# Waiting for the last two stores on the queues that issued them, in a one-token attention and MLP layer

## The chip, the cores and the metric

The kernel runs on one core of a Trainium2 chip. The metric is the device time of one execution in microseconds (us). Before the change it is 100.47 us, the median of three runs that lie between 100.42 and 100.51 us.

## The reference

One token `x` of 1024 values goes through a layer norm, and then through two branches whose results are added to it: grouped attention with 32 query heads and 4 key and value heads over the last 4096 positions of a cache, and an MLP with 3584 hidden units that has a second layer norm of its own. Everything is stored in bf16.

```python
W = min(4096, max(256, Sk // 4))                     # 4096 of 65536 positions
q = (x @ wq).reshape(B, Sq, Hq, Dh)                  # 32 heads of 128
k, v = k_cache[:, :, Sk - W:, :], v_cache[:, :, Sk - W:, :]   # each head repeated 8 times
p = softmax(q @ k.T * Dh ** -0.5)
A = (p @ v).reshape(B, Sq, Hq * Dh) @ wo
B = gelu(layernorm(x) @ w1 + b1) @ w2 + b2
out = x + A(xn) + B(xn)                              # xn = layernorm(x)
```

## The kernel before

The work is bound to weights and caches that are read once: 39.86 MB come from HBM, and the output is one row of 1024 values. Four SBUF buffers (`slot`) are loaded in turn by SyncE (SP): the key window, `wq`, the two halves of `w1`, the value window, the two halves of `w2`, and at the end the 32 rows of `wo` in pieces. TensorE (PE) multiplies the rows as they land. VectorE (DVE) and ScalarE (ACT) transpose and copy the keys, and VectorE adds most rows of `w2` up. GpSimd (POOL) builds masks in the first part and is not needed for arithmetic after that.

The end of the work goes like this. The last rows of `wo` land, 32 small matmuls (line 227, with helper loads at line 219) add them into the PSUM tile `acc`, VectorE copies 288 columns of it to the SBUF tile `res` (line 569) and ScalarE the other 224 (line 570). Then two DMAs of 1 KB each write the output: one half is issued by SyncE (`out0`) and the other half by ScalarE (`out1`), both by the helper whose `dma_start` call is at line 213. They are the last two operations of the plan, and their numbers are given to `emit` as `done`.

`Plan.emit` turns a list of operations into instructions with semaphores. Each engine has a counter (`pe_count`, `dve_count` and so on) that it raises when an operation on which another engine depends is finished. Each DMA has a semaphore of its own that is 16 when all of it has landed. At the end, GpSimd sets all of them back to zero, so that the program can run again:

- at line 111 it waits until VectorE's and ScalarE's counters have their last values, which is when `res` is complete;
- at line 112 it clears the list `used`: all semaphores of loads and the counters of PE, GpSimd and SyncE;
- at lines 113 and 114 it waits for the two stores;
- at line 115 it clears the list `ends`: the counters of VectorE and ScalarE and the semaphores of the two stores.

SyncE and ScalarE have nothing more to do after they issued their stores, and VectorE and PE, whose instructions are put in blocks of their own behind this (`dve_main`, `pe_main`), have nothing after `res` and the last matmul.

Of the kernel before, what the change touches and what calls it, by code (L numbers as in the profile page):

```python
# [14 lines left out]
class Plan:  # L15
# [11 lines left out]
    def emit(self, done):  # L27
        nc, ops = self.nc, self.ops
        writer, readers, deps = {}, {}, []
        for n, (eng, fn, r, w, dma, over) in enumerate(ops):  # L30
            need = set()
            for k in over:
                need.update((m, False) for m in readers.get(k, ()))
            for k in r:
                if k in writer:
                    need.add((writer[k], True))
            for k in w:
                if k in writer:
                    need.add((writer[k], True))
                need.update((m, False) for m in readers.get(k, ()))  # L40
            keep = set()
            for m, after_write in need:
                if m == n:
                    continue
                same = ops[m][0] == eng and ops[m][4] is None and dma is None
                if same and (eng == "pe" or not after_write):
                    continue
                keep.add(m)
            deps.append(keep)
            for k in r:  # L50
                readers.setdefault(k, []).append(n)
            for k in w:
                writer[k] = n
                readers[k] = []
        clock = {e: {} for e in self.engines}
        snap, waits, ordinal, count = [], [], [], {e: 0 for e in self.engines}
        for n, (eng, fn, r, w, dma, _) in enumerate(ops):
            c, mine = clock[eng], []
            for m in sorted(deps[n], reverse=True):
                lane = ("dma", m) if ops[m][4] is not None else ops[m][0]  # L60
                if c.get(lane, -1) >= ordinal[m]:
                    continue
                mine.append(m)
                for key, v in snap[m].items():
                    if c.get(key, -1) < v:
                        c[key] = v
                c[lane] = max(c.get(lane, -1), ordinal[m])
            waits.append(mine)
            ordinal.append(count[eng])
            count[eng] += 1  # L70
            snap.append(dict(c))
        wanted = {m for mine in waits for m in mine if ops[m][4] is None}
        wanted.update(m for m in range(len(ops)) if m in done)
        sems = {e: nc.alloc_semaphore(f"{e}_count") for e in ("pe", "pool", "sp")}
        used, ends = list(sems.values()), []
        value, ticks = {}, {e: 0 for e in self.engines}
        for e in ("dve", "act"):
            sems[e] = nc.alloc_semaphore(f"{e}_count")
            ends.append(sems[e])
        for n in done:  # L80
            value[n] = (nc.alloc_semaphore(f"dma{n}"), 16)
            ends.append(value[n][0])
        for n, (eng, fn, r, w, dma, _) in enumerate(ops):
            if dma is not None:
                if n in done:
                    continue
                value[n] = (nc.alloc_semaphore(f"dma{n}") if dma is True else dma, 16)
                used.append(value[n][0])
            elif n in wanted:
                ticks[eng] += 1  # L90
                value[n] = (sems[eng], ticks[eng])

        def put(n):
            eng, fn, r, w, dma, _ = ops[n]
            lanes = {}
            for m in waits[n]:
                s, v = value[m]
                if id(s) not in lanes or lanes[id(s)][1] < v:
                    lanes[id(s)] = (s, v)
            for s, v in lanes.values():  # L100
                self.engines[eng].wait_ge(s, v)
            i = fn()
            if i is not None and n in value:
                i.then_inc(value[n][0], value[n][1] if dma is not None else 1)

        own = [("dve", mybir.EngineType.DVE), ("pe", mybir.EngineType.PE)]
        for n, o in enumerate(ops):
            if o[0] not in ("dve", "pe"):
                put(n)
        for e in ("dve", "act"):  # L110
            nc.gpsimd.wait_ge(sems[e], ticks[e])
        nc.clear_and_free_semaphores(used)
        for s, v in [value[m] for m in done]:
            nc.gpsimd.wait_ge(s, v)
        nc.clear_and_free_semaphores(ends)
        never = {}
        for e, _ in own:
            never[e] = self.engines[e].alloc_register(f"{e}_never")
            self.engines[e].reg_mov(never[e], 0)
            self.engines[e].br(f"{e}_main")  # L120
        for e, kind in own:
            nc.enter_bb(f"{e}_main", valid_engines=[kind])
            back = self.engines[e].mark_branch_hint_location()
            for n, o in enumerate(ops):
                if o[0] == e:
                    put(n)
            self.engines[e].br_eq(never[e], 1, f"{e}_main", f"{e}_last").branch_hint(back)
            nc.enter_bb(f"{e}_last", valid_engines=[kind])
            self.engines[e].nop()
# [475 lines left out]
```

## Time and profile before

| | us |
|---|---|
| median of three runs | 100.47 (100.42 to 100.51) |
| the profiled execution, its own time | 100.62 |
| the profiled execution, span from the first to the last instruction of the kernel | 98.83 |
| time of that execution that lies around the span | 1.79 |
| last matmul of `acc` raises PE's counter, from the span's start | 96.93 |
| SyncE issues its store | 97.38 to 97.65 |
| ScalarE issues its store | 97.40 to 97.88 |
| ScalarE's store has landed | 98.50 |
| SyncE's store has landed | 98.68 |
| GpSimd's last clear (line 115) | 98.79 to 98.83 |

The page of the profile lists busy time by engine; instructions that only wait, branch, clear semaphores or issue DMAs are not counted as busy and stand in the views by line with a q behind the engine's name (SPq, POOLq). The landing times are from the trace's records of semaphore updates: a store's semaphore reaches its full value there.

The records of semaphore updates go on after the kernel's last instruction. The kernel's own semaphores have the numbers 99 to 129. Number 2 isn't one of them; it is raised in groups of nine, once just before the kernel's first instruction, once around its end, and once after all semaphores have been set back to zero. The prediction calls these updates marks.

### The profile page before, as it was taken

How to read it: one execution, taken by the hardware profiler on the slowest of the kernel's cores; microseconds unless marked ns; L12 is line 12 of the kernel's file. 1: busy time of each engine (PE TensorE's matmuls, PEld its weight loads, DVE VectorE, ACT ScalarE, POOL GpSimd, SP SyncE). 2: the span in 40 equal slices, each digit the busy share in tenths (PEclk: the TensorE clock that was granted, in tenths of full speed). 3: DMA queues.
4: the chain of work that ended last, by engine and by line, in shares of the span. 5: the costliest groups of instructions: out<-in, count | busy, mean ns of one | idle time of the engine just before them, and what ended most of it. 6: DMA issues, size and time to landing. Idle time of an engine off the chain costs nothing.

```text
span 98.8 us, 961 instructions
## 1 busy us (share of the span) xinstructions
PE 57.2 (58%) x323; PEld 16.2 (16%) x220; DVE 73.9 (75%) x75; ACT 30.7 (31%) x29; POOL 10.0 (10%) x22
## 2 busy tenths in 40 slices
PE   0032040598200699960899586667670999594792
PEld 0022000123000233410202121212210111110130
DVE  0023776999999999999102677899999999999431
ACT  0050000089999899992001075100000000000001
POOL 0072580000000680000000000000000000000000
PEclk9999999999985556997558999999999589999999
DMA  3999979999999999999799999999998999999970
GB/s 50 448 418 451 464 328 458 441 511 438 424 424 405 395 453 453 395 441 464 338 424 424 418 441 413 463 424 429 487 418 383 431 431 424 424 424 405 405 265 1
DMA packets 3132, 39.86 MB, mean 403 GB/s; under 512 B 438, under 2 KB 444, under 8 KB 828
## 3 DMA queue, kind: packets, MB, share of 16 engines
q1 hardware_dynamic: 3082, 39.86, 95.4%
q10 hardware_dynamic: 50, 0.00, 0.0%
HBM read 39.86 MB, written 0.00 MB: 403 GB/s over the span
## 4 chain that ended last, share of the span: by engine, by line
DVE 36%; DMA 32%; PE 20%; issue 5%; SPq 2%; ACT 2%; DVEq 0%
DMA slot<-in_A_wo_dram 20%; DVE slot L334 18%; DVE kT L343 13%; DMA slot<-in_A_k_cache_dram 13%; PE qo_ps L495 10%; PE sc_ps L227 6%; PE acc L227 2%; SPq L194 2%; ACT e L450 1%; DVE eTb L454 1%; DVE m_loc L435 1%; PE acc L233 1%; DVE q_sb L388 1%; ACT sc L427 1%; DVE res L569 0%
## 5 line engine op out<-in xcount | busy, mean ns | idle before, releaser
L339 ACT COPY kT<-slot 32x1024 bf16<-32x1024 bf16 (+1 forms) x18 | 23.9, 1327 | 14.3 <-DVE slot L334 14.1
L482 DVE SCALAR_TENSOR_TENSOR run<-slot,hTf,run 128x1024 f32<-128x1024 bf16 x20 | 24.2, 1272 | 0.0
L369 PE MATMUL acc<-slot,xw 128*128 x48 | 15.7, 494 | 12.6 <-DMA slot<-in_A_wq_dram 12.2
L334 DVE STREAM_TRANSPOSE slot<-slot 128x4096 bf16<-128x4096 bf16 x4 | 17.4, 4414 | 1.2 <-DMA slot<-in_A_k_cache_dram 1.2
L343 DVE COPY kT<-slot 32x4096 bf16<-32x4096 bf16 x10 | 13.2, 1316 | 0.2
L495 PE MATMUL qo_ps<-slot,eTb 128*128 (+1 forms) x32 | 10.2, 382 | 5.1 <-issue 4.0
L227 PE MATMUL sc_ps<-slot,o 128*1 128x512 bf16 x48 | 9.1, 378 | 2.8 <-DMA slot<-in_A_wo_dram 2.8
L369 PEld LDWEIGHTS acc<-slot,xw 128*128 x48 | 5.5, 115 | 23.5 <-issue 21.1
L570 ACT CAST res<-acc 33x224 bf16<-33x224 f32 x1 | 0.3, 338 | 20.1 <-PE acc L227 20.1
L227 PE MATMUL sc_ps<-kT,qm 128*32 128x512 bf16 x32 | 6.1, 973 | 0.3 <-DVE qm L416 0.3
L495 PEld LDWEIGHTS qo_ps<-slot,eTb 128*128 (+1 forms) x32 | 3.1, 96 | 12.0 <-issue 8.7
L428 DVE COPY sc<-sc_ps 128x512 f32<-128x512 f32 x1 | 0.7, 691 | 5.7 <-PE sc_ps L227 5.7
L227 PE MATMUL sc_ps<-slot,hT 128*1 128x512 bf16 x14 | 4.7, 509 | 0.1
L538 ACT CAST o<-misc 128x32 bf16<-128x32 f32 x1 | 0.2, 186 | 14.6 <-PE misc L233 14.6
L219 PEld LDWEIGHTS <-o 128*1 128x1 bf16 x40 | 2.4, 83 | 12.4 <-issue 11.8
L233 PE MATMUL misc<-x,spread 32*128 32x8 bf16 x4 | 0.3, 168 | 6.2 <-POOL spread L255 6.2
L249 DVE MEMSET mhalf<- 128x1 f32 x1 | 0.1, 59 | 5.0 <-PEq L203 5.0
L233 PE MATMUL acc<-spread,qm 32*128 32x512 bf16 x4 | 1.6, 498 | 3.7 <-POOL qm L315 3.7
L227 PE MATMUL acc<-slot,yT 128*1 128x448 bf16 x64 | 3.4, 353 | 0.0
L427 ACT COPY sc<-sc_ps 128x512 f32<-128x512 f32 x1 | 0.6, 585 | 8.8 <-PE sc_ps L227 8.8
L251 ACT ACT_TABLE_LOAD x1 | 1.3, 1283 | 4.8 <-PEq L203 4.8
L227 PE MATMUL acc<-slot,o 128*1 128x288 bf16 (+1 forms) x32 | 2.2, 272 | 0.6 <-DMA slot<-in_A_wo_dram 0.6
(88 smaller groups left out, 46.0 us busy)
## 6 DMA issues: line engine op xcount, KB each, us to landing
slot<-in_B_w_dram SPq DMA_DIRECT2D x3, 3584.0 KB, 16.6
slot<-in_A_wo_dram SPq DMA_DIRECT2D x3, 2048.0 KB, 22.8
slot<-in_A_k_cache_dram SPq DMA_DIRECT2D x4, 1024.0 KB, 9.8
slot<-in_A_wq_dram SPq DMA_DIRECT2D x1, 4096.0 KB, 27.0
slot<-in_A_v_cache_dram SPq DMA_DIRECT2D x1, 4096.0 KB, 16.1
slot<-in_A_wq_dram SPq DMA_DIRECT2D x2, 1024.0 KB, 9.2
slot<-in_A_wq_dram SPq DMA_DIRECT2D x1, 2048.0 KB, 17.8
slot<-in_B_w_dram SPq DMA_DIRECT2D x1, 2048.0 KB, 21.5
```

The source lines that it names most:

```text
L194: return nc.sync.dma_start(out=k_sb[g:P - Hkv + g + 1:Hkv, :], in_=A_k_cache[0, g, Sk - W:Sk, :].rearrange("(r c) d -> r (c d)", r=P // Hkv))
L219: return pe.add_instruction(mybir.InstLdweights(name=nc.get_next_instruction_name(), engine=i.engine, tile_size=(P, 32), tile_position=pos ...
L227: return pe.add_instruction(mybir.InstMatmult(name=nc.get_next_instruction_name(), engine=i.engine, start_tensor_calc=start, stop_tensor_c ...
L233: op("pe", lambda: pe.matmul(out_ap, lhsT=w_ap, rhs=x_ap, start=start, stop=stop, tile_position=pos), r, w)
L251: op("act", lambda: act.activation(out=dummy[:, 0:1], in_=mhalf[0:1, 0:1], func=ACT.Exp), ("mhalf",), ("act_warm",))
L334: op("dve", lambda s=s: dve.transpose(out=scr[:, s, :], in_=k2[:, s, :]), ("k0", "k1", "k2", "k3", "slot0"), (f"scr{s}",))
L339: op("act", lambda s0=s0, s1=s1, R=R, Cd=Cd: act.copy(out=kT[32 * Cd:32 * Cd + 32, R, s0:s1, :].rearrange("p s (c j) -> p (s c) j", j=32), ...
L343: op("dve", lambda R=R, Cd=Cd: dve.tensor_copy(out=kT[32 * Cd:32 * Cd + 32, R, :, :].rearrange("p s (c j) -> p (s c) j", j=32), in_=T3[32 ...
L369: pe.matmul(acc2[:, b, :], lhsT=xw[:, bass.ds(32 * n + 512 * i, P)], rhs=slot[1 + i][:, bass.ds(1024 * n + 512 * b, 512)], start=False, st ...
L427: op("act", lambda: act.copy(out=sc[:, 512:1024], in_=sc_ps[:, 1, :]), ("sc1",), ("scs1",))
L482: op("dve", lambda: dve.scalar_tensor_tensor(out=t, in0=wap, scalar=hTf[:, c:c + 1], in1=t, op0=ALU.mult, op1=ALU.add), (key, "hTf", f"run ...
L495: return pe.matmul(qo_ps, lhsT=cols, rhs=v4[:, :, c, :], start=first, stop=last)
```

## The change

The semaphores of the two stores leave the list that GpSimd clears, and a new semaphore, `left`, enters it. SyncE and ScalarE each raise `left` by one right behind the instruction that issues their store. GpSimd no longer waits for the stores: it waits until `left` is 2, and then clears VectorE's and ScalarE's counters and `left`. SyncE and ScalarE each get one more instruction at their end, which waits until the engine's own store has landed (16) and takes the 16 back from the semaphore.

```diff
         for e in ("dve", "act"):
             sems[e] = nc.alloc_semaphore(f"{e}_count")
             ends.append(sems[e])
+        left = nc.alloc_semaphore("left")
+        ends.append(left)
         for n in done:
             value[n] = (nc.alloc_semaphore(f"dma{n}"), 16)
-            ends.append(value[n][0])
...
         nc.clear_and_free_semaphores(used)
-        for s, v in [value[m] for m in done]:
-            nc.gpsimd.wait_ge(s, v)
+        for n in done:
+            self.engines[ops[n][0]].sem_inc(left, 1)
+        nc.gpsimd.wait_ge(left, len(done))
         nc.clear_and_free_semaphores(ends)
+        for n in done:
+            s, v = value[n]
+            self.engines[ops[n][0]].wait_ge(s, v).then_inc(s, -v)
```

## The prediction

> **What bounds the kernel now.** I read the page first, then the chain of waits, then the timeline of the last microseconds, and last the lines that the diff touches.
>
> The page and the end of the chain of waits (start, length, what):
>
> ```profile
> span 98.8 us, 961 instructions
> ...
> DMA  3999979999999999999799999999998999999970
> ...
> 74.51 19.40 DMA slot<-in_A_wo_dram
> ...
> 96.86 0.45 DVE res L569
> ```
>
> The transfers are busy up to the last two slices; nothing that the diff touches can move them. The chain of the view ends with `res` at 97.31 us. What follows is the part that the diff touches: 1.52 us up to the end of the span at 98.83, and 1.79 us more that the profiled execution took (100.62) than its span.
>
> The timeline of that part (start, length, engine, line):
>
> ```profile
> 96.95 0.34 ACT L570 CAST res<-acc 33x224 bf16<-33x224 f32 x1 [20.07 <-PE acc L227]
> 97.38 0.27 SPq L213 DMA_DIRECT2D out_dram<-res  x1
> 97.40 0.48 ACTq L213 DMA_DIRECT2D out_dram<-res  x1
> ```
>
> The lines of GpSimd's end (durations in ns, then the start in us):
>
> ```profile
> L112 POOLq EVENT_SEMAPHORE_RANGE_CLEAR  x2: 92/112/132, 97.5 to 97.7; - x2
> L114 POOLq EVENT_SEMAPHORE  x1: 17/17/17, 98.5 to 98.5; - x1
> L115 POOLq DRAIN  x1: 55/55/55, 98.7 to 98.7; - x1
> L115 POOLq EVENT_SEMAPHORE_RANGE_CLEAR  x1: 47/47/47, 98.8 to 98.8; - x1
> ```
>
> GpSimd stands from 97.85 us on for the two stores. ScalarE's lands at 98.504 and GpSimd's wait at line 114 starts 0.024 later; SyncE's lands at 98.678, the drain that carries its wait starts 0.024 later (98.702 to 98.757), and the clear runs from 98.786 to 98.833. So 0.155 us lie between the last landing and the end of the span.
>
> The rest is in the records of semaphore updates, semaphore 2, in us from the span's start:
>
> ```
> marks before the kernel   -0.371 -0.337 -0.299 -0.255 -0.231 -0.120 -0.081 -0.047  0.000
> marks at its end          97.089 98.147 99.354 99.399 99.422 99.519 99.559 99.593 99.639
> marks after the clearing 100.429 100.464 100.502 100.546 100.569 100.668 100.706 100.740 100.787
> ```
>
> The first and third rows run freely, with steps of 0.02 to 0.11 us. The second row doesn't: its first mark comes 0.161 us after PE's counter got its last update (96.928), its second 0.272 after ScalarE had issued its store (97.875), its third 0.521 after GpSimd's last clear (98.833), and from there the steps are the free ones (0.045 against 0.044, 0.023 against 0.023). I read the marks as a round of the five engines in a fixed order, there and back, in which each adds its mark when it is done and has seen the one before: PE, ScalarE, GpSimd, then VectorE and SyncE in the two remaining places, SyncE at the turn, and back. That SyncE turns is inferred: it is the first engine with an instruction in the kernel, at 0.00. All other semaphores are cleared behind the fifth to ninth mark, and the last row follows. So **GpSimd's last clear and its walk of 0.521 us to the third mark set the end**; the time from the fifth mark (99.422) to the last update (100.787), 1.365 us, hangs behind it.
>
> The Trainium skill, page "Runtime: NRT & Kernel Launch", section "The ~15µs preamble/postamble breakdown", describes such a round of the five engines (44 ns a hop), here 0.371 us for eight steps, and gives about 1.5 us for waiting there until all engines are done. Here 0.81 us pass from GpSimd's last clear to the ninth mark. Taken as a fixed price behind the last instruction, whichever engine has it, its rule would leave only the shift of the span's end; that shift is worked out as a rival below.
>
> **The change part by part.**
>
> *Raising `left`.* Two instructions, on SyncE and ScalarE, behind the issue of the store. The stores themselves aren't moved or delayed. The nearest rows are the waits of these engines:
>
> ```profile
> L203 SPq EVENT_SEMAPHORE  x2: 17/17/17, 4.4 to 4.7; - x2
> L203 ACTq EVENT_SEMAPHORE  x2: 17/17/17, 4.4 to 4.7; - x2
> ```
>
> They take 0.017 us, and 0.05 to 0.09 us from start to the start of what follows. SyncE is free at 97.646 and ScalarE at 97.875, and each would stand until its landing at 98.678 and 98.504. The cover is over 0.6 us, so the cost is nothing; without cover it would be at most 0.09.
>
> *GpSimd's end.* `left` is 2 at about 97.875 + 0.06 + 0.017 = 97.95. Then come 0.024, the drain and the clear (98.833 - 98.702 = 0.131): the end is at 98.11, in place of 98.833. With the walk of 0.521 GpSimd reaches its mark at 98.63. The first clears of line 112 end at 97.85 and stay where they are; the list has two runs of numbers as before. GpSimd is no longer last.
>
> *SyncE's and ScalarE's last instructions.* Each is a wait that also takes the value back; the two rows above are of this form (they wait for and lower a semaphore), 0.017 us. Nothing of the kernel is queued behind them; only the marks wait for them. ScalarE: 98.504 + 0.024 + 0.017 = 98.545. SyncE: 98.678 + 0.024 + 0.017 = **98.719**, which becomes the last instruction of the kernel.
>
> *The walk from there to the mark.* This is the disputed size. GpSimd's is 0.521, ScalarE's 0.272, PE's 0.161 from its last update. SyncE's isn't seen: it is free at 97.646 and has only to have marked by 99.422, so anything up to 1.776 us would have been hidden. By the rows it stands between 0.161 and 0.521. I take ScalarE's 0.272, for two reasons. In the barrier at line 203 SyncE and ScalarE keep the same pace (0.092 us from a wait to the next drain on both, 0.072 and 0.076 from the second wait to what follows). And their drains take 7 and 8 ns where GpSimd's take 34 to 184, which would lengthen a walk that contains some:
>
> ```profile
> L203 POOLq DRAIN  x2: 34/38/41, 0.8 to 4.4; - x2
> L112 POOLq DRAIN  x2: 70/76/82, 97.4 to 97.6; - x2
> L589 SPq DRAIN  x1: 7/7/7, 0.0 to 0.0; - x1
> L589 ACTq DRAIN  x1: 8/8/8, 0.1 to 0.1; - x1
> ```
>
> **The sum.** SyncE's mark, the fifth: 98.719 + 0.272 = 98.991. What is late next is ScalarE: 98.545 + 0.272 = 98.817, and three free steps (0.038, 0.045, 0.023) bring it to 98.923 at the fifth mark. GpSimd's 98.63 is behind ScalarE's mark. So SyncE's own arrival sets the fifth mark, at 98.991 in place of 99.422: **0.43 us less**, of which the span shows only 0.11. Behind it 1.365 us follow as now. The profiled execution of 100.62 becomes 100.19; it lies 0.15 above the median of the runs, so the forecast for the median is 100.47 - 0.43 = **100.04 us**.
>
> **Bounds.** With PE's 0.161 for both walks, SyncE marks at 98.880: 0.54 less, 99.93 us. With GpSimd's 0.521 it marks at 99.240: 0.18 less, 100.29 us. If VectorE turned and SyncE stood fourth, one step of 0.023 would be added. The runs before spread by 0.04 to each side.
>
> **The rivals.**
>
> 1. *Every engine's walk is about GpSimd's, when it comes out of a last wait for a store* (chance 0.15). ScalarE's walk was seen only behind a DMA issue, not behind a wait. For it: GpSimd is the only engine whose walk began at such a wait. Against it: drains on GpSimd are dearer. The gain is 0.18 us, 100.29. The neighbouring reading, a fixed time behind the kernel's last instruction, gives 98.833 - 98.719 = 0.11 less, 100.36. Both are hardly to be told from no change.
> 2. *SyncE's walk is long, and its stand hid it* (chance 0.08). The mechanism: SyncE must now begin, 1.07 us later than today (98.719 against 97.646), a way to the mark that has always lain under GpSimd's wait. It decides from a walk of 0.70 us on (99.422 - 98.719); there the change gains nothing. At the limit of what today's trace can hide, 1.776 us, the mark would be at 100.495, 1.07 late: 101.54 us. In the middle of that, 1.24, it is 0.54 late, 101.01. For it: no row of SyncE's walk exists. Against it: its pace in the barrier rows is ScalarE's.
> 3. *The change doesn't do what it says* (chance 0.05): the raise of `left` waits for the store on one of the engines, or the wait and the taking back fall apart into more instructions, with GpSimd's clear again behind the landing. Then GpSimd's walk sets the end as now: 100.47, at most 0.1 to either side.
> 4. *Both walks are shorter than PE's row* (chance 0.02): below 99.93 us.
>
> **How the numbers follow.** The forecast has 0.70. A measurement of this kernel can tell about 0.2% from no change, 0.20 us. Faster by more than that: the forecast and case 4, 0.72. Within it: cases 1 and 3, 0.20. Slower: case 2, 0.08. The range takes in the forecast with its bounds and case 1's own 0.18, with 0.04 for the spread of the runs: from 99.93 - 0.04 = 99.89 to 100.29 + 0.04 = 100.33 us.
>
> **What would show it.** In the profile of the changed kernel: GpSimd's last clear near 98.1 us; a wait of SyncE at about 98.7 as the last instruction, so a span only 0.11 shorter while the time falls by about 0.43; the third mark no longer 0.52 behind GpSimd's clear but a free step behind the second; the fifth mark 0.27 behind SyncE's wait. The prediction is wrong if that last distance is over 0.5 us, if a store lands later than 1.3 us after its issue, or if the marks follow the span's end at the old distance.

## The result, and the profile after

The changed kernel takes **99.93 us** (median of five runs, 99.84 to 99.95) against 100.51 us of the kernel before beside it (100.42 to 100.67): a ratio of 0.9939 with a 95% interval of 0.9925 to 0.9954, so 0.6% faster. The forecast was 100.04 us, 0.43 less than before; 0.58 was measured. All ratios here are to the kernel before, run beside, and leave out the few executions that took over 1.5% longer than the fastest of their kernel.

The page, the end of the chain of waits and the timeline (start, length, engine and line) of the changed kernel:

```profile
span 98.6 us, 964 instructions
...
DMA  3999979999999899889799999999998999999970
```

```profile
75.74 20.58 DMA slot<-in_A_wo_dram
...
96.69 0.45 DVE res L574
```

```profile
97.21 0.27 SPq L218 DMA_DIRECT2D out_dram<-res  x1
97.23 0.48 ACTq L218 DMA_DIRECT2D out_dram<-res  x1
```

The profiled executions differ ahead of the change too: `res` begins 0.17 us earlier here, and 0.14 us of that stand already at the first transposes (15.44 in place of 15.58 us). The diff touches nothing there. Therefore everything below is counted from PE's last update of its counter, behind the last matmul (96.928 us before, 96.761 after). From there the stores are issued at 0.45 and 0.47 us in both kernels.

The lines of the changed end (durations in ns, then the start in us): the two raises of `left`, GpSimd's last clear, and the two waits that take a semaphore back.

```profile
L115 SPq EVENT_SEMAPHORE  x1: 17/17/17, 97.5 to 97.5; - x1
L115 ACTq EVENT_SEMAPHORE  x1: 17/17/17, 97.7 to 97.7; - x1
```

```profile
L117 POOLq DRAIN  x1: 62/62/62, 97.8 to 97.8; - x1
L117 POOLq EVENT_SEMAPHORE_RANGE_CLEAR  x1: 46/46/46, 97.9 to 97.9; - x1
```

```profile
L120 ACTq EVENT_SEMAPHORE  x1: 17/17/17, 98.4 to 98.4; - x1
L120 SPq EVENT_SEMAPHORE  x1: 17/17/17, 98.5 to 98.5; - x1
```

GpSimd's last clear has moved from 98.8 to 97.9 us, ahead of both landings, and the kernel's last instruction is SyncE's wait at 98.54. Each new instruction takes 17 ns. The marks, from the records of semaphore 2, in us from PE's last update, in the kernel before, the changed one, and a second run of the changed one:

```
              mark:  1     2     3     4     5     6     7     8     9   last update
before             0.161 1.219 2.426 2.471 2.494 2.591 2.631 2.665 2.711  3.859
after              0.160 1.756 1.794 1.838 1.943 1.987 2.025 2.059 2.106  3.257
after, again       0.161 1.758 1.796 1.840 1.945 1.989 2.027 2.061 2.108  3.260
```

The third mark, which hung on GpSimd, is now a free step (0.038) behind the second, and the second comes 0.140 us behind the end of ScalarE's wait (1.616). The fifth comes 0.146 behind the end of SyncE's wait (1.797), and 0.105 behind the fourth, where 0.023 is the free step: SyncE is the last to arrive. The last update comes 0.60 us earlier, about the measured gain of 0.58, while the kernel's last instruction ends only 0.11 us earlier (1.797 in place of 1.905).

That the last update stands for the program's time can be read from the profiles. In nine of the twelve of this document the execution's own time is 0.167 to 0.183 us less than the time of its last update from the span's start (100.62 against 100.787 before, 99.84 against 100.018 after). The exceptions are three kernels of the experiments: with one store on SyncE (0.04 less), with one store on ScalarE (0.64 more) and with both waits on TensorE (0.75 more).

### The profile page after: what moved, and what is told of

The parts are those of the page before. It is cut to its first block, busy times and chain, and to the rows that moved or that the text cites. A ratio compares the mean times of both kernels' runs of the same rounds, so it can differ in the third digit from the quotient of the medians.

```text
span 98.6 us, 964 instructions
## 1 busy us (share of the span) xinstructions
PE 57.2 (58%) x323; PEld 16.2 (16%) x220; DVE 73.9 (75%) x75; ACT 30.8 (31%) x29; POOL 9.9 (10%) x22
## 4 chain that ended last, share of the span: by engine, by line
DVE 36%; DMA 33%; PE 18%; issue 5%; SPq 4%; ACT 2%; DVEq 0%
DMA slot<-in_A_wo_dram 21%; DVE slot L339 18%; DVE kT L348 13%; DMA slot<-in_A_k_cache_dram 12%; PE qo_ps L500 10%; PE sc_ps L232 6%; SPq L199 2%; SPq L218 2%; ACT e L455 1%; DVE eTb L459 1%; DVE m_loc L440 1%; DVE q_sb L393 1%; ACT sc L432 1%; DVE res L574 0%; SPq L204 0%
```

## The experiments

The way from an engine's last instruction to its mark is called its walk, as in the prediction. Theory A: GpSimd walks about 0.52 us from its last instruction to its mark, whatever that instruction is; ScalarE and SyncE walk about 0.15. So what counts is which engine handles the last landing. Theory B: the 0.52 us belong to the clear that was GpSimd's last instruction. A further rival is that each half of the change has its own share. All diffs are against the changed kernel and cut to the lines that matter, and the marks are counted from PE's last update as above.

**GpSimd takes the stores back itself** (e1_pool_takes).

```diff
-        for n in done:
+        for n in reversed(done):
             s, v = value[n]
-            self.engines[ops[n][0]].wait_ge(s, v).then_inc(s, -v)
+            nc.gpsimd.wait_ge(s, v).then_inc(s, -v)
```

> GpSimd clears the counters while the stores fly, as in the changed kernel, but GpSimd itself then waits for both stores and takes their semaphores back; SyncE and ScalarE only raise left. No clear is behind the landing. Theory A (the walk to the mark depends on the engine, and GpSimd's is about 0.52 us after any last instruction): GpSimd's last wait ends 0.04 us after the last landing and its mark, the third, comes 0.52 us later; against the kernel before only the drain and the clear are saved, about 0.1 us, so -0.1%. Theory B (the 0.52 us belong to the clear that was GpSimd's last instruction): the mark comes about 0.15 us after the wait, as on SyncE and ScalarE in the changed kernel, and some 0.48 us are saved, -0.5%.

Measured: ratio 0.9985 (0.9956 to 1.0014), the last update at 3.801 us. The lines of GpSimd's end in this kernel:

```profile
L117 POOLq EVENT_SEMAPHORE_RANGE_CLEAR  x1: 46/46/46, 97.9 to 97.9; - x1
...
L120 POOLq EVENT_SEMAPHORE  x2: 17/17/17, 98.4 to 98.6; - x2
```

The clear is early, exactly as in the changed kernel, and the two waits are 17 ns each; but the second ends at 1.806 and the third mark comes at 2.371, 0.565 later. By the marks only 0.06 us of the 0.60 are gained, and the ratio can't tell that from nothing. Theory A holds, and B falls: clearing the counters while the stores fly is nearly worthless as long as GpSimd is the one that waits.

**One half of the change at a time** (e2_sp_part_alone, e3_act_part_alone). One engine takes its own store back; the other store's semaphore is waited for and cleared by GpSimd.

```diff
             value[n] = (nc.alloc_semaphore(f"dma{n}"), 16)
+        ends.append(value[done[1]][0])        # done[0] in the other run
...
-        for n in done:
-            self.engines[ops[n][0]].sem_inc(left, 1)
-        nc.gpsimd.wait_ge(left, len(done))
+        mine, its = done[0], done[1]          # done[1], done[0] in the other run
+        self.engines[ops[mine][0]].sem_inc(left, 1)
+        nc.gpsimd.wait_ge(left, 1)
+        nc.gpsimd.wait_ge(*value[its])
         nc.clear_and_free_semaphores(ends)
-        for n in done:
-            s, v = value[n]
-            self.engines[ops[n][0]].wait_ge(s, v).then_inc(s, -v)
+        s, v = value[mine]
+        self.engines[ops[mine][0]].wait_ge(s, v).then_inc(s, -v)
```

> SyncE waits for its own store and takes its semaphore back; GpSimd still waits for ScalarE's store and clears it with the other counters. Theory A and B alike: GpSimd's clear ends 0.155 us after ScalarE's landing, which is 0.17 us before SyncE's, and the third mark 0.52 us behind it: about 0.17 us less than before, -0.17%. If the whole gain came from what SyncE does, it would be 0.6 us, -0.6%.

> ScalarE waits for its own store and takes its semaphore back; GpSimd still waits for SyncE's store and clears it with the other counters. GpSimd's clear ends 0.155 us after the last landing as before, and the third mark 0.52 us behind it: no difference, 0.0%, within 0.05 us. If each half of the change had its own share, the two halves alone would add up to 0.6 us, and this one would bring some 0.4.

Measured: with SyncE's half alone a ratio of 1.0009 (0.9978 to 1.0041), with ScalarE's half alone 0.9981 (0.9941 to 1.0022). GpSimd's end in the two kernels, SyncE's half first:

```profile
L119 POOLq DRAIN  x1: 55/55/55, 98.2 to 98.2; - x1
L119 POOLq EVENT_SEMAPHORE_RANGE_CLEAR  x1: 47/47/47, 98.3 to 98.3; - x1
```

```profile
L119 POOLq DRAIN  x1: 55/55/55, 98.7 to 98.7; - x1
L119 POOLq EVENT_SEMAPHORE_RANGE_CLEAR  x1: 47/47/47, 98.8 to 98.8; - x1
```

GpSimd clears behind the landing that is left to it, and its third mark follows 0.521 us behind the clear in both (1.783 to 2.304, and 1.974 to 2.495). The last update is 0.12 us earlier than before with SyncE's half and 0.07 later with ScalarE's, where the wait for the store is now an instruction of its own ahead of the drain (it was part of the drain before). The runs can't tell the 0.12 from nothing; that figure rests on one profile. The two halves don't add up: -0.12 and +0.07 alone, -0.60 together. The gain comes only when GpSimd waits for no store at all.

**Both stores taken back by one engine** (e4 ScalarE, e5 SyncE, e8 VectorE, e9 TensorE). The two waits stand at the end of that engine's stream, for VectorE and TensorE at the end of their own blocks.

```diff
-        for n in done:
+        for n in reversed(done):
             s, v = value[n]
-            self.engines[ops[n][0]].wait_ge(s, v).then_inc(s, -v)
+            self.engines["act"].wait_ge(s, v).then_inc(s, -v)      # "sp"; "dve" and "pe" behind the nop
```

> As the changed kernel, but ScalarE takes both semaphores back and SyncE only raises left. It tests the order of the round of marks. Theory (ScalarE stands second and SyncE fifth): ScalarE's mark comes about 0.18 us after SyncE's landing, and three steps, 0.1 to 0.2 us, follow before the round has got as far as in the changed kernel: 0.15 us more than the changed kernel, 0.45 less than before, -0.45%. Rival (the place in the round doesn't matter, each engine's mark counts once): as the changed kernel, -0.6%.

> As the changed kernel, but SyncE takes both semaphores back and ScalarE only raises left; the counterpart of the run with both on ScalarE, which ended 0.14 us later than the changed kernel. Theory (SyncE's landing and walk alone set the end, and SyncE stands late in the round): as the changed kernel, -0.6%, the last update of semaphore 2 about 3.26 us after PE's last (before: 3.86, changed kernel: 3.26); ScalarE's mark early. Rival (a second wait on SyncE delays its mark, or ScalarE's landing had its own part in the end): 0.05 us to either side of that.

> As the changed kernel, but VectorE takes both semaphores back, at the end of its own block; SyncE and ScalarE only raise left. It asks whether GpSimd alone has a dear walk. Theory (GpSimd's 0.52 to 0.57 us is its own, the other engines walk in about 0.15 us behind such a wait): VectorE's mark, the fourth, comes about 0.15 us after its last wait, that is 1.95 us after PE's last update, and the last update of semaphore 2 at about 3.3 (changed kernel 3.26, before 3.86), -0.55% against before. Rival (ScalarE and SyncE are the quick ones, since they are the engines that issue DMAs, and every other engine walks like GpSimd): the fourth mark 0.52 us after the wait, at 2.32, the last update at 3.7, -0.15%.

> As the changed kernel, but TensorE takes both semaphores back, at the end of its own block. Theory (its walk is about 0.16 us, as behind its last matmul, and it stands first, so the whole round follows): first mark at 1.95 us after PE's last update, the last update of semaphore 2 at about 3.45, 0.2 later than the changed kernel, -0.4% against before. Rival (every engine but ScalarE and SyncE walks like GpSimd): first mark at 2.32, the last update at 3.85, 0.0%.

Measured, with the walk from the end of the last wait to the engine's own mark (that of GpSimd from the first experiment beside them):

```
engine     its mark   last wait ends   mark    walk    sixth mark   last update   ratio to before
ScalarE    2          1.791            1.931   0.140   2.133        3.399         0.9936 (0.9905 to 0.9967)
SyncE      5          1.791            1.934   0.143   1.978        3.248         0.9927 (0.9893 to 0.9960)
VectorE    4          1.796            1.978   0.182   2.099        3.366         0.9962 (0.9941 to 0.9983)
TensorE    1          1.835            2.069   0.234   2.305        3.854         0.9959 (0.9937 to 0.9981)
GpSimd     3          1.806            2.371   0.565   2.535        3.801         0.9985 (0.9956 to 1.0014)
```

The lines of the waits: VectorE's take 21 ns, TensorE's 51.

```profile
L135 DVEq EVENT_SEMAPHORE  x2: 21/21/21, 98.4 to 98.6; - x2
```

```profile
L135 PEldq EVENT_SEMAPHORE  x2: 51/51/51, 98.5 to 98.7; - x2
```

In each run the mark that came late was that of the engine that was given the waits, and the marks behind it up to the fifth followed in free steps (0.02 to 0.05). So the order in the round, which the prediction had inferred, is shown: TensorE, ScalarE, GpSimd, VectorE, SyncE. GpSimd alone has a walk of over 0.5 us; the others take 0.14 to 0.23. And the place matters too: the same landing on ScalarE, second in the round, gives a sixth mark 0.155 us later than on SyncE. The rival that the place doesn't matter falls by the marks (the ratios of the two, 0.9936 and 0.9927, overlap). TensorE's mark came at 2.069, 0.12 us behind the theory's 1.95 and 0.25 ahead of the rival's 2.32, and the ratio is the theory's. But the last update of its profile came at 3.854, where the theory had 3.45 and the rival 3.85. Of the 0.40 us beyond the theory only 0.12 come from the late mark; the rest lies between the ninth mark and the next row, where 1.07 us pass and in ten of the twelve profiles 0.79. That profile is of an execution that took 101.50 us where the median is 100.48, and no instruction of the kernel is left in that stretch; what the 0.28 us are stays open.

**One store in place of two** (e6 SyncE, e7 ScalarE).

```diff
-    out_v = out.rearrange("a b (t s n) -> t (a b) s n", t=2, s=16)
-    dma("sp", out_v[0], res[0:1, :].rearrange("a (s n) -> a s n", s=16), ("res_a", "res_b"), ("out0",))
-    dma("act", out_v[1], res[32:33, :].rearrange("a (s n) -> a s n", s=16), ("res_a", "res_b"), ("out1",))
-    plan.emit([len(plan.ops) - 2, len(plan.ops) - 1])
+    dma("sp", out.rearrange("a b (t n) -> t (a b n)", t=2), res[0:33:32, :], ("res_a", "res_b"), ("out0",))   # "act"
+    plan.emit([len(plan.ops) - 1])
```

> Both halves of the output in one store of two rows, issued by SyncE, which waits for it and takes it back; ScalarE issues none. Theory (the end hangs on SyncE's landing, and its packet ran 0.05 us behind ScalarE's on the same chip resource): the packet starts up to 0.05 us earlier and the landing comes 0.05 to 0.1 us earlier, so the last update of semaphore 2 comes at about 3.17 to 3.21 us after PE's last, against 3.26 in the changed kernel, -0.65 to -0.7% against before. Rival (two rows in one store take longer to issue and to land than one): the landing is 0.1 to 0.3 us later and all of it is seen at the end, -0.3 to -0.5%.

> Both halves in one store of two rows, issued by ScalarE, which waits for it and takes it back; SyncE issues none. Theory (ScalarE's store lands 1.11 us after the start of its issue against 1.30 on SyncE, its walk is 0.14 us as on SyncE, but it stands second in the round, which costs about 0.14): landing at 1.11 or earlier, mark at 1.75 after PE's last update, last update of semaphore 2 at about 3.2 us, about as the changed kernel, -0.6%. Rival (ScalarE's landing was early only because SyncE's store shared the work): landing at 1.3 as on SyncE, last update at 3.4, -0.45%.

Measured: on SyncE a ratio of 0.9946 (0.9918 to 0.9975), on ScalarE 0.9959 (0.9928 to 0.9991). The timelines of the two kernels:

```profile
97.09 0.59 SPq L218 DMA_DIRECT2D out_dram<-res  x1
```

```profile
97.09 1.06 ACTq L218 DMA_DIRECT2D out_dram<-res  x1
```

The rival was right for SyncE. The issue of two rows takes 0.59 us on SyncE where one row took 0.27, and 1.06 on ScalarE where one took 0.48; the landing comes 1.62 us after the start of the issue on both (1.31 and 1.11 with one row each). In the kernel with SyncE the whole 0.31 us are seen at the end: last wait at 2.106 in place of 1.797, fifth mark at 2.248 in place of 1.943, last update at 3.562 in place of 3.257. How long the issue lasts doesn't set the landing by itself, since it is the same behind 0.59 and 1.06 us. The records of the transfers show more: the first packet starts 1.21 us after the start of the issue on both engines, against 0.79 (SyncE) and 0.72 (ScalarE) with one row. On SyncE the last packet starts 0.46 us later than with one row, and the landing follows 0.37 us behind it in place of 0.52. So it may be that the other store's packet had cost SyncE's landing up to 0.15 us, as my theory wanted; the later packets outweigh that.

With ScalarE the last update was missed by both the theory and the rival. The second mark comes at 2.276, 0.146 behind the wait, and the last update of that profile at 3.892, no earlier than before the change, where the theory had 3.2 and the rival 3.4. Of this, 0.15 us lie again between the ninth mark and the next row (0.94 us), in an execution that took 101.15 us where the median is 100.34; without them it would be 3.75. The ratio says 0.4% less, with an interval that reaches to 0.1%.

**The changed kernel once more** (after_again).

> The changed kernel once more, for comparison on the same chip: -0.6% against before; the last update of semaphore 2 at 3.26 us after PE's last, SyncE's and ScalarE's walks 0.14 to 0.15 us.

Measured: 0.9942 (0.9915 to 0.9969); its marks stand above. No version beats it: both waits on SyncE give the same within what was measured (0.9927 against 0.9942, last update 3.248 against 3.260).

## Why the prediction was right, and where its terms were off

The time lies in the range (99.89 to 100.33), near its lower end, and the mechanism is the forecast one: the last landing was taken from GpSimd, and most of the gain is the shorter walk. Of the 0.60 us at the last update, 0.375 are SyncE's 0.146 in place of GpSimd's 0.521, 0.108 the drain and the clear that no longer stand behind the landing, 0.068 the two steps from the third to the fifth mark, which no longer follow the last arrival, and 0.051 the distance behind the fifth mark. The gain of 0.58 us is more than the 0.54 that the prediction gave with PE's row for both walks. Step by step, for the profiled pair, counted from PE's last update:

- *Raising `left` costs nothing.* Right: 17 ns each, 0.58 us or more ahead of the landings, and the stores are issued at the same 0.45 and 0.47 us.
- *GpSimd's last clear near 98.1 us, its mark out of the way.* Right: the clear ends 1.17 us after PE's last update; 98.11 would have been 1.18.
- *SyncE's last instruction at the landing plus 0.041.* Right: predicted 1.791 (98.719 less 96.928), measured 1.797. The landing was 0.014 us later, and the wait ended 0.033 behind it in place of 0.041.
- *SyncE's walk of 0.272.* **This is the term that was off**: 0.146, and 0.140 on ScalarE. It accounts for 0.126 of the missing 0.17 us. The row that I took it from, ScalarE's second mark behind its store's issue, isn't a walk alone. In three runs (both waits on GpSimd, SyncE or VectorE) ScalarE's last instruction is the raise of `left`, which ends 0.05 us behind the issue, and the mark still comes 0.267 to 0.274 us behind the issue's recorded end. That points to something of the issue, and not to the last instruction, as what the row hangs on. The records show the first update of the store's semaphore 0.08 to 0.09 us behind that end, and the mark 0.185 to 0.191 behind the update; what the mark waits for there isn't shown. In the kernel where ScalarE issues nothing its second mark comes 0.116 behind its copy of `res`, and behind a wait it is 0.140. PE's 0.161 was no lower bound either: TensorE walked 0.234 when the wait was given to it, and in the runs with both waits on GpSimd and on VectorE the same row is 0.326.
- *The time behind the fifth mark stays at 1.365.* Off by 0.05 us: it is 1.314. A late fifth mark is not paid in full. When the fifth came 0.023 behind the fourth, the sixth followed 0.097 later; when it came 0.105, 0.187 and 0.406 behind the fourth (the changed kernel, both waits on SyncE, one store on SyncE), the sixth followed 0.044 later in all three. These figures fit a sixth mark that waits for the fourth plus 0.12 as well as for the fifth plus 0.04.

Sum: -0.431 predicted, +0.006 for the wait, -0.126 for the walk, -0.051 behind the fifth mark, together -0.60; measured at the last update, -0.602.

The rivals. That every walk behind a wait is GpSimd's 0.52 (chance 0.15) is refuted by every engine but GpSimd itself: 0.14 to 0.23. The neighbouring reading, a fixed time behind the last instruction of the kernel, falls with it: from that instruction to the ninth mark 0.81 us passed before and 0.31 in the changed kernel, 0.85 with GpSimd waiting. The prediction had named as its source the 1.5 us that the Trainium skill, page "Runtime: NRT & Kernel Launch", section "The ~15µs preamble/postamble breakdown", gives for waiting until all engines are done; no run here shows a fixed time of that kind, and the three just named are all shorter. That SyncE's stand hid a long walk (0.08) is refuted by four runs with 0.14 to 0.15 us. That the change doesn't do what it says (0.05) is refuted by the line of GpSimd's clear at 97.9. The case of two walks shorter than PE's row (0.02) is what the marks show, and the median of 99.93 stands at its border; that chance was too small, since its bound came from an engine whose mark I had seen only behind a matmul.

Not settled: why GpSimd's walk is 0.52 to 0.57 us. Its drains take 34 to 184 ns where those of the other engines mostly take 7 to 10, as the prediction argued, but no record shows what lies between its last instruction and its mark, and no experiment took that apart. That ScalarE's walk behind an issue is longer than behind a wait is shown; why is open too.

## What to carry to other kernels

Look past the span: the program's end here is a round through all engines, and the last wait of this kernel is best given to an engine with a short way to its mark, and late in that round. Moving work off an engine gains nothing while that engine still waits for the last landing; both halves of this change were worth nothing that could be measured alone. A distance that is counted from the end of an issue row may hold something of the issue itself; it can't stand for the way behind another kind of instruction.

## What the runs showed of the hardware that I had not expected

- The way from an engine's last wait to its mark: SyncE 0.142 to 0.146 us, ScalarE 0.139 to 0.146, VectorE 0.182, TensorE 0.234, GpSimd 0.565 (0.521 to 0.536 behind its clear).
- The round's sixth mark, VectorE's second, came 0.12 us or more behind its first in every run; a late SyncE is partly hidden under that.
- A store of two 1 KB rows took SyncE 0.59 us to issue against 0.27 for one row, ScalarE 1.06 against 0.48, and landed 1.62 us after the start of its issue on either (1.31 and 1.11 with one row).
